# Two more weight tiles between the attention loop and the first gather, issued by GpSimd

## The chip, the cores and the metric

The kernel runs on one core of a Trainium2 chip. The metric is the device time of one execution in microseconds (us). The engines of the core are TensorE (PE; its weight loads are PEld), VectorE (DVE), ScalarE (ACT), GpSimd (POOL) and SyncE (SP); transfers run on 16 DMA engines, fed by a hardware queue (q1, issued by SyncE here) and a software queue (q0, issued by GpSimd).

## The reference

Eight batches of eight heads run an attention with a block-causal mask (576 tokens, head size 64, blocks of 64); the result, 4608 tokens of 512, goes through a mixture of eight experts, of which each token uses one, and each expert keeps at most 80 tokens.

```python
attn = softmax(where(block_i >= block_j, q @ k.T / 8, -1e9)) @ v     # (8, 8, 576, 64)
x = attn.transpose(0, 2, 1, 3).reshape(4608, 512)
logits = x @ w_gate                                                  # 8 experts
expert_idx, gate_w = argmax(logits), softmax(logits) at the argmax
for e in range(8):
    tok_idx = the 80 tokens of expert e with the largest gate_w
    out[tok_idx] = gate_w[tok_idx] * (relu(x[tok_idx] @ w1[e]) @ w2[e])
```

All other rows of the output are zero.

## The kernel before

**The loop.** Two heads make a pair; 32 pairs are taken through the turns of a loop that is written out by hand (lines 40 to 166): loads five turns ahead, transposes, scores, maxima, exponentials (`soft`), transposed probabilities (`back`), values, and the transposition of the result (`flip`). The tables give the order on every engine. The exponentials lie in two sets of tiles, `Pt[0]` and `Pt[1]`, used by even and odd pairs in turn, so the last pair, 31, uses `Pt[1]`. The last turn (table `LAST`) holds only the second half of pair 31's work: its scores and exponentials are made in the turn before. After each batch of four pairs its part of `xs`, the tokens in DRAM, is stored by SyncE (lines 387 to 393), and GpSimd makes a product `sp` (line 463) that TensorE turns (line 472) and VectorE copies to the table `Wt` (line 478), from which the tokens are selected. The product of the last batch but one comes after the loop (`while not turns: t()`, line 770), that of the last batch is made by VectorE.

**The weights.** Each expert has an up tile (`w1`) and a down tile (`w2`) of 2 MB; 16 tiles in the order of `wlist` (line 316): up 0, up 1, down 0, up 2, down 1, up 3, down 2, up 4 and so on. Three buffers (`wp`) are filled during the loop, by GpSimd in DMAs of 512 and 256 KB (line 332). Three more (`fwa`) lie in the memory that the loop's pools of the right side used; they come after `att.close()`. The later ones (`fwc`, `fwb`) come after the selection, and from the tenth tile on buffers are used again. Before the change one tile, up 2, is sent by SyncE (line 337) between the loop and the first gather, behind the stores of the last batch. All further ones wait for the second gather (`fetches[HOLD]`, lines 1019 and 1024).

**The selection and the experts.** VectorE and GpSimd find 80 tokens for each expert; the list is `gi` (line 924). GpSimd issues eight gathers (`xg`, line 934) from `xs`; VectorE divides (`xn`, line 1032), TensorE transposes (line 1052), multiplies with the up tile (line 1043) and the down tile (line 1096), VectorE scales (line 1100) and GpSimd scatters (line 1105). While the selection runs, TensorE is kept busy with filling matmuls on `identr` (line 680). Behind the loop the order on the engines is set by a scheduler, except where `issue_after` ties two instructions.

```python
    for e in range(E):
        fetch = pool.indirect_dma_start(
            out=xg[e], out_offset=None, in_=xs[:, :],
...
    weights(1, fetches[HOLD])
```

Of the kernel before, what the change touches and what calls it, by code (L numbers as in the profile page):

```python
# [7 lines left out]
F32 = mybir.dt.float32  # L8
# [10 lines left out]
P = 128  # L19
BLK = 64  # L20
NT = 5
FW0, FWA, FWC, FWB = 3, 3, 1, 2
WARM = [8, 12, 6, 9, 24]
START_WARM = 6
NCAND = 12
# [7 lines left out]
WIDE = {"78": 512, "56": 512, "34": 320, "12": 256, "08": 3 * BLK}  # L33
# [136 lines left out]
def tile_attn_moe(ctx, tc, q, k, v, w_gate, w1, w2, capacity, out, xs=None, dbg=None):  # L170
    nc = tc.nc
    B, H, S, D = q.shape
    NTOK, DM = out.shape
    E, _, F = w1.shape
# [20 lines left out]
    att = ExitStack()  # L195
    right = dict(side="right")
    pb = att.enter_context(tc.tile_pool(name="pb", bufs=1, **right))
# [38 lines left out]
    def clear(i, eng=nc.gpsimd):  # L236
        if ov is not None:
            if 0 <= i < nz:
                return eng.dma_start(ov[i], zero.rearrange("p (r d) -> p r d", r=2))
        elif i == 0:  # L240
            for j in range(NTOK // BLK):
                nc.sync.dma_start(out[j * BLK:(j + 1) * BLK, :], zero[0:BLK, 0:DM])
# [62 lines left out]
    def constants3():  # L305

        nc.vector.tensor_tensor(iota_c16, sameR, iota_c, op=ALU.mult)
        nc.vector.tensor_reduce(iota_r, iota_c16, axis=AX.X, op=ALU.add)
        nc.gpsimd.tensor_copy(cf, ci)
        nc.vector.scalar_tensor_tensor(cap, cf[:, 1:2], 4294967296.0, cf[:, 0:1], op0=ALU.mult, op1=ALU.add)  # L310
        nc.vector.tensor_tensor(caplt, iota_p, cap, op=ALU.is_lt)

    nw, loaded = 0, None
    wpools = [wp] * FW0
# [4 lines left out]
    def weights(n, after=None):  # L319
        for _ in loads(n, after):  # L320
            pass

    def loads(n, after=None):

        nonlocal nw, loaded
        for _ in range(n):
            src, e = wlist[nw]
            w_ = wpools[nw % len(wpools)].tile([P, KP * F], F32, name="w")
            nw += 1
            wt_[src is w2, e] = w_ = w_.rearrange("p (a f) -> p a f", f=src.shape[2])  # L330
            if nw <= FW0:
                yield from (nc.gpsimd.dma_start(w_[:, a], src[e][a * P:(a + 1) * P]) for a in range(w_.shape[1]))
                continue
            with ExitStack() as order:
                if loaded is not None:
                    order.enter_context(tc.issue_after(loaded.ins))
                load = loaded = nc.sync.dma_start(w_, src[e].rearrange("(a p) f -> p a f", p=P))
            if after is not None:
                tc.add_manual_dep(load.ins, after.name, mybir.DependencyInfo(
                    mybir.DependencyClass.Sync, mybir.DependencyReason.DATA))  # L340

    Pt = [{u: pb.tile([P, 2, w], F32, name=f"P{u}_{i}") for u, w in WIDE.items()} for i in range(2)]

    QT = [pb.tile([P, S], F32, name=f"qt{i}") for i in range(2)]

    VT = [pb.tile([P, 2, D], F32, name=f"vt{i}") for i in range(4)]

    ld = att.enter_context(tc.tile_pool(name="ld", bufs=4, **right))  # L350
    qk = att.enter_context(tc.tile_pool(name="qk", bufs=2, **right))
    attp = ExitStack()
    psp = [attp.enter_context(tc.tile_pool(name=f"psp{i}", bufs=1, space=PSUM)) for i in range(8)]

    def banks(use, where=BANKS):
        return [psp[i].tile([P, 512], F32, name=f"bank{i}") for i in where[use]]
# [134 lines left out]
    class Pair:  # L491
# [11 lines left out]
        def load(self):  # L503

            b, h0 = self.b, self.h0
            self.nat = [ld.tile([P, S // 32, 32], F32, name=f"ld{x}") for x in range(2)]
            for x in (0, 1) if self.i < 2 else (1, 0):
                for h in range(2):
                    for i in range(2):
                        r = slice(h * D + 32 * i, h * D + 32 * i + 32)  # L510
                        eng = nc.sync
                        if h == 1 and (self.i == 0 or x == 1 and self.i > 4):
                            eng = nc.gpsimd if self.i else nc.scalar
                        eng.dma_start(self.nat[x][r], (q, k)[x][b, h0 + h, :, 32 * i:32 * i + 32]  # L514
                                                      .rearrange("(g r) d -> r g d", r=32))

        def load_v(self):
# [3 lines left out]
            for h in range(2):  # L521
                eng.dma_start(self.vn[:, h], v[b, h0 + h, 0:512].rearrange("(j p) d -> p j d", p=P))  # L522
            self.vt = VT[self.i % 4]
            eng.dma_start(self.vt[BLK:P], v[b, h0:h0 + 2, 512:576].rearrange("h p d -> p h d"))

        def prep(self, x):
# [3 lines left out]
            if x == 1:  # L530
                self.T[1] = t
                return
            self.T[0] = q_ = QT[self.i % 2]
            tb, qb = (y.rearrange("p (b r) -> p b r", r=BLK) for y in (t, q_))
# [137 lines left out]
    def warm(n, wt, after=None):  # L672

        if not n:
            return
        with ExitStack() as order:
            if after is not None:
                order.enter_context(tc.issue_after(after.ins))
            for i in range(n):
                nc.tensor.matmul(wt.rearrange("p (a c) -> p a c", c=P), lhsT=identr,  # L680
                                 rhs=identr.unsqueeze(1).broadcast_to([P, 4, P]), start=(i == 0), stop=(i == n - 1))
# [50 lines left out]
    late = ExitStack()  # L732
    tw = dict(reuse_waits="tile")
# [4 lines left out]
    with tc.manual_schedule():  # L738
        warm(WARM[0], banks("g")[0])
        early = loads(FW0)  # L740
        for i in range(-LEAD, n):
            if i == -1:
                nc.sync.dma_start(ci, capacity.bitcast(U32).partition_broadcast(P))
                for h in range(2):
                    nc.sync.dma_start(wgd[h * D:(h + 1) * D, :, h * E:(h + 1) * E], wg_v[h])

            for _ in range(min(4, nz - kept - cleared) if i >= n - 5 else 0):
                clear(cleared, nc.sync)
                cleared += 1
            if i == 1 - LEAD:  # L750
                nc.scalar.activation(early_exp, ramp[:, 2, 0:1], AF.Exp)
                constants()
            if i == -1:
                constants2()
            if i == 1:
                constants3()
            if i >= 2 and i % 3:
                next(early, None)
            for d, what, *args in FIRST if i == -1 else AHEAD if i == -2 else TURN if i < n - 1 else LAST:
                if what in slots_:  # L760
                    slots_[what]()
                elif 0 <= i + d < n and not (what == "flip" and n - NP <= i + d < n - 2):
                    getattr(pairs[i + d], what)(*args)
            if n - NP <= i + valued < n - 2:
                pairs[i + valued].flip()
            if i >= flipped and (i - flipped) % NP == NP - 1 and i - flipped < n - 1:
                enqueue(batches[(i - flipped) // NP])
        for _ in early:
            pass
        while not turns:  # L770
            t()
        bt = batches[B - 1]
        pairs[n - 2].flip()
        for _ in bt.recip():
            pass
        bt.store_sums()
        to, from_ = pairs[n - 1].out.pop("V0")
        pairs[n - 1].take("V1", "v")
        nc.scalar.copy(to[:, 0], from_[:, 0])
        nc.vector.tensor_copy(to[:, 1], from_[:, 1])  # L780
        att.close()
        fwa = late.enter_context(tc.tile_pool(name="fwa", bufs=FWA, **right, **tw))
        wpools += [fwa] * FWA
        lt = bt.logits_of()
        pairs[n - 1].flip()
        bt.store_x()
        weights(1)
        bt.logits_out(lt)
        bt.logits2()
        bt_, mark = turns.pop(0)  # L790
        bt_.turn2(banks("av")[0])
        mark()
        for _ in (*bt.products(), *bt.shift()):
            pass
        bt.expo()
        while small:
            t()
        found, weighed = bt.first_of(), bt.weight()
        for g_ in (found, found, found, weighed, found, weighed, weighed):
            next(g_)  # L800
        bt.turn(nc.vector, 2)
        bt.turn2(banks("L")[0])
        for _ in bt.placed():
            pass
# [8 lines left out]
    pool = nc.gpsimd  # L813
# [50 lines left out]
    HOLD = 1  # L864
# [64 lines left out]
    xg, fetches = [], []  # L929
# [10 lines left out]
    for k, ins in enumerate((bt_.last, bt.last, ranked, picked)):  # L940
        warm(WARM[1 + k], wt[:, k % 2], ins)

# [77 lines left out]
    with tc.issue_after(loaded.ins):  # L1020
        while cleared < nz:
            loaded = clear(cleared, nc.sync)
            cleared += 1
    weights(FWA - 2 + FWC + FWB, fetches[HOLD])

    def divide(dst, src):

# [296 lines left out]
```

## Time and profile before

| what | us |
|---|---|
| median of 3 runs | 396.84 (396.63 to 399.62) |
| the profiled execution | 397.45, of it the span of the trace 395.7 |
| busy: TensorE, VectorE, ScalarE, GpSimd | 374.4, 285.3, 290.7, 171.9 |
| moved by DMA | 84.40 MB, 213 GB/s on the mean |

The span goes from the first to the last instruction. Busy times are sums over the span; a busy TensorE need not be at its peak. A "share" of DMA is the mean busy share of the 16 engines; in loaded stretches it reaches a little over 1. Where a share is multiplied by the length of its stretch, the unit is called share-us. Rows of stretches give the stretch, its length, the busy us (and instructions) of PE, PEld, DVE, ACT and POOL, the granted clock of TensorE (1.00 is 2.4 GHz), the DMA share and GB/s. In rows of a timeline the first number is the start from the span's start, the second the length; in brackets stands the idle time of the engine ahead of it and what ended it.

### The profile page before, as it was taken

The page shows a single profiled execution, that of the slowest core. Times are in us where ns is not written, and L with a number is a line of the kernel's source. Part 1 is how long each engine was busy: PE and PEld are TensorE (multiplying, and loading weights), DVE is VectorE, ACT ScalarE, POOL GpSimd, SP SyncE. Part 2 cuts the span into 40 slices and gives each one's busy share as a digit, 9 for nine tenths or more (in the row PEclk, how much of TensorE's full clock was granted, in tenths as well). Part 3 has the DMA queues.
Part 4 walks back from the last instruction along what each step waited for, and adds up shares of the span by engine and source line. Part 5 has one row for each costly group of instructions (what it writes and reads, how often), then busy time and mean ns, then how long its engine had stood idle before and what let it go on. Part 6 is the DMA issues. An engine that isn't in the chain of part 4 may idle for free. (4 is left out here: it accounts for less than half of the span.)

```text
span 395.7 us, 15123 instructions
## 1 busy us (share of the span) xinstructions
PE 374.4 (95%) x5963; PEld 254.8 (64%) x5963; DVE 285.3 (72%) x812; ACT 290.7 (73%) x886; POOL 171.9 (43%) x333
## 2 busy tenths in 40 slices
PE   5899999999999999999999999998899899999991
PEld 3566766766766766766667667666578745666551
DVE  5879899999999998999999999999764220100000
ACT  1799999999999999999999999999122122333231
POOL 6246664575665567556467544510147010000010
PEclk9999999999999999999999999999999999999997
DMA  9979999899999999999999998999477999999801
GB/s 125 151 125 189 137 183 180 167 214 111 186 170 241 161 136 235 156 156 214 129 153 213 176 151 170 374 383 272 104 244 226 355 398 397 393 398 395 306 22 36
DMA packets 169917, 84.40 MB, mean 213 GB/s; under 512 B 132573, under 2 KB 151869, under 8 KB 169840
## 3 DMA queue, kind: packets, MB, share of 16 engines
q1 hardware_dynamic: 158352, 61.80, 72.5%
q0 software_dynamic: 9120, 21.27, 23.4%
q8 instruction: 49, 0.80, 1.0%
q10 hardware_dynamic: 2368, 0.30, 0.6%
q14 instruction: 28, 0.23, 0.3%
HBM read 63.21 MB, written 20.33 MB: 211 GB/s over the span
## 5 line engine op out<-in xcount | busy, mean ns | idle before, releaser
L600 ACT ACTIVATE P<-bank,negm 128x512 f32<-128x512 f32 (+3 forms) x320 | 158.7, 583 | 11.1 <-DVE negm L589 6.2
L553 PE MATMUL bank<-T,qt 64*128 64x320 f32 (+3 forms) x512 | 98.7, 495 | 1.0 <-DVE PT L670 0.8
L589 DVE TENSOR_REDUCE negm<-bank 128x1 f32<-128x320 f32 (+2 forms) x192 | 83.7, 475 | 8.5 <-PE bank L579 8.4
L652 PE MATMUL bank<-PT,vn 128*64 128x64 f32 (+3 forms) x1280 | 88.1, 293 | 0.6 <-ACT PT L670 0.6
L670 ACT COPY PT<-bank 128x512 f32<-128x512 f32 x158 | 82.6, 669 | 3.6 <-PE bank L634 3.2
L536 POOL TENSOR_SCALAR qt<-T 128x128 f32<-128x128 f32 (+2 forms) x96 | 31.1, 341 | 106.6 <-DVE T L529 106.6
L652 PEld LDWEIGHTS bank<-PT,vn 128*64 128x64 f32 x1280 | 56.3, 137 | 27.1 <-ACT PT L670 4.1
L600 ACT ACTIVATION_READ_ACCUMULATOR P<-bank,negm 128x1 f32 x256 | 70.8, 276 | 0.0
L634 PEld LDWEIGHTS bank<-ident,P 64*128 64x128 f32 (+1 forms) x1600 | 58.9, 137 | 11.9 <-issue 6.3
L634 PE MATMUL bank<-ident,P 64*128 64x64 f32 (+1 forms) x1600 | 64.7, 226 | 1.1 <-ACT P L600 0.6
L553 PEld LDWEIGHTS bank<-T,qt 64*128 64x128 f32 x512 | 46.8, 187 | 27.8 <-ACT PT L670 14.5
L589 DVE TENSOR_REDUCE raw<-bank 128x1 f32<-128x64 f32 (+1 forms) x128 | 52.5, 445 | 2.4 <-PE bank L553 1.6
L529 DVE STREAM_TRANSPOSE T<-ld 128x576 f32<-128x576 f32 x64 | 49.6, 774 | 3.0 <-DMA ld<-in_q_dram 1.7
L522 POOL DMA_DIRECT2D vn<-in_v_dram x58 | 46.0, 799 | 1.6 <-PE bank L658 1.1
L1100 DVE SCALAR_TENSOR_TENSOR y<-av,comb,yt 80x512 f32<-80x512 f32 (+1 forms) x8 | 5.6, 696 | 51.5 <-ACT yt L1099 50.7
L1043 PE MATMUL ps<-xsT,w 128*64 128x80 f32 x1024 | 38.7, 234 | 2.4 <-issue 1.8
L1043 PEld LDWEIGHTS ps<-xsT,w 128*64 128x64 f32 x1024 | 36.6, 137 | 6.0 <-issue 4.7
L1105 POOL DMA_INDIRECT out_dram<-y,si x8 | 7.4, 926 | 74.2 <-DVE y L1100 74.2
L1096 PE MATMUL av<-w,hT 128*32 128x512 f32 (+3 forms) x320 | 39.1, 553 | 0.0
L514 POOL DMA_DIRECT2D ld<-in_k_dram x54 | 37.5, 704 | 3.5 <-DMA ld<-in_q_dram 2.9
L1099 ACT ACTIVATE yt<-ps,gfar 32x512 f32<-32x512 f32 (+2 forms) x18 | 11.4, 635 | 26.0 <-PE ps L1096 25.8
L1066 ACT ACTIVATE hT<-ps 128x320 f32<-128x320 f32 x16 | 7.0, 437 | 30.6 <-PE ps L1043 30.6
(177 smaller groups left out, 435.3 us busy)
## 6 DMA issues: line engine op xcount, KB each, us to landing
w<-in_moe_w_dram SPq DMA_DIRECT2D x13, 2048.0 KB, 21.6
xs<-Y SPq DMA_DIRECT2D x32, 288.0 KB, 5.8
out_dram<-zero SPq DMA_DIRECT2D x18, 512.0 KB, 7.6
ld<-in_q_dram SPq DMA_DIRECT2D x126, 72.0 KB, 5.5
vn<-in_v_dram POOLq DMA_DIRECT2D x58, 128.0 KB, 5.4
ld<-in_k_dram SPq DMA_DIRECT2D x72, 72.0 KB, 5.2
w<-in_moe_w_dram POOLq DMA_DIRECT2D x8, 512.0 KB, 7.2
ld<-in_k_dram POOLq DMA_DIRECT2D x54, 72.0 KB, 6.1
```

What stands on the lines that cost most here:

```text
L514: eng.dma_start(self.nat[x][r], (q, k)[x][b, h0 + h, :, 32 * i:32 * i + 32] .rearrange("(g r) d -> r g d", r=32))
L522: eng.dma_start(self.vn[:, h], v[b, h0 + h, 0:512].rearrange("(j p) d -> p j d", p=P))
L529: nc.vector.transpose(t, self.nat[x].rearrange("p g d -> p (g d)"))
L536: nc.gpsimd.tensor_scalar(qb[:, to], tb[:, of], scalar1=SCALE, scalar2=1.0, op0=ALU.mult, op1=ALU.mult)
L553: nc.tensor.matmul(s[h][:, c:c + n], lhsT=q_[:, P * t - BLK:P * t + BLK], rhs=k_[:, 0:n], start=(c == 0 and g != "2"), stop=(g == "1"))
L589: nc.vector.tensor_reduce(to[:, b, h:h + 1], self.s[g][h][:, c:c + n], axis=AX.X, op=ALU.max, negate=True)
L600: nc.scalar.activation(Pt[self.i % 2][u][:, h, c1:c1 + n], self.s[g][h][:, c:c + n], AF.Exp, bias=self.negm[:, t, h:h + 1], scale=1.0, acc ...
L634: nc.tensor.transpose(pt[c][0:cols.stop - cols.start, n_ * BLK:(n_ + 1) * BLK], row[u][r, h, cols], ident[r, r])
L652: nc.tensor.matmul(a4[r] if c0 is None else av[r, BLK * c0:BLK * (c0 + b1 - b0)], lhsT=self.vn[:, h, j, :], rhs=self.PT[:, h, row, b0:b1]. ...
L670: (nc.scalar.copy if (eng or TAKE[x]) == "a" else nc.vector.tensor_copy)(*self.out.pop(x))
L1043: yield nc.tensor.matmul(dst(b)[64 * c:64 * (c + 1)], lhsT=w_[:, a, col:col + 64], rhs=x_[:, a], start=(a == 0), stop=(a == n - 1))
L1096: last = nc.tensor.matmul(to[col:col + s1 - s0, c0:c1], lhsT=hT[:, a, s0:s1], rhs=w_[:, a, c0:c1], start=(a == ends[0]), stop=(a == ends[1 ...
```

## The change

The weights function lets GpSimd issue the first five tiles instead of the first three (`FW0 + SOON`, with `SOON = 2`). The two more, up 2 and down 1, are issued right behind the loop, ahead of `while not turns: t()`. For this the loop's right-side pools are closed there, and laid out in another order: first the tiles that are read for the last time in the last turn but one (`Pt[0]`, `QT`, the loaded q and k, their transposes `T`), then, in the pools `ld` and `pb1`, the values and `Pt[1]`, which the last turn still reads. SyncE's single tile behind the last batch's stores is now up 3. Behind the gathers two tiles fewer are sent.

```diff
+SOON = 2
...
-            if nw <= FW0:
+            if nw <= FW0 + SOON:
                 yield from (nc.gpsimd.dma_start(w_[:, a], src[e][a * P:(a + 1) * P]) for a in range(w_.shape[1]))
                 continue
...
-    Pt = [{u: pb.tile([P, 2, w], F32, name=f"P{u}_{i}") for u, w in WIDE.items()} for i in range(2)]
-
+    def turned(i, pool):
+        return {u: pool.tile([P, 2, w], F32, name=f"P{u}_{i}") for u, w in WIDE.items()}
+
+    Pt = [turned(0, pb)]
     QT = [pb.tile([P, S], F32, name=f"qt{i}") for i in range(2)]
 
-    VT = [pb.tile([P, 2, D], F32, name=f"vt{i}") for i in range(4)]
-
+    nats = att.enter_context(tc.tile_pool(name="nats", bufs=4, **right))
+    qk = att.enter_context(tc.tile_pool(name="qk", bufs=2, **right))
     ld = att.enter_context(tc.tile_pool(name="ld", bufs=4, **right))
-    qk = att.enter_context(tc.tile_pool(name="qk", bufs=2, **right))
+    pb1 = att.enter_context(tc.tile_pool(name="pb1", bufs=1, **right))
+    Pt.append(turned(1, pb1))
+    VT = [pb1.tile([P, 2, D], F32, name=f"vt{i}") for i in range(4)]
...
-            self.nat = [ld.tile([P, S // 32, 32], F32, name=f"ld{x}") for x in range(2)]
+            self.nat = [nats.tile([P, S // 32, 32], F32, name=f"ld{x}") for x in range(2)]
...
         for _ in early:
             pass
+        att.close()
+        fwa = late.enter_context(tc.tile_pool(name="fwa", bufs=FWA, **right, **tw))
+        wpools += [fwa] * FWA
+        weights(SOON)
         while not turns:
             t()
...
         nc.vector.tensor_copy(to[:, 1], from_[:, 1])
-        att.close()
-        fwa = late.enter_context(tc.tile_pool(name="fwa", bufs=FWA, **right, **tw))
-        wpools += [fwa] * FWA
         lt = bt.logits_of()
...
-    weights(FWA - 2 + FWC + FWB, fetches[HOLD])
+    weights(FWA - SOON - 2 + FWC + FWB, fetches[HOLD])
```

GpSimd's instructions at the end of the loop, before the change (`qt` is the scaled q of the last pair, `sp` the product of the last batch but one):

```order
L536 TENSOR_SCALAR qt_143<-T_5571 128x128
L536 TENSOR_SCALAR qt_143<-T_5571 128x64
L536 TENSOR_SCALAR qt_143<-T_5571 128x384
L463 TENSOR_TENSOR sp<-Gm,sameE 128x320
L892 CAST RI<-sameE 128x12x8
```

The same place after the change, from the second of the new DMAs on, with the counters that each waits for (DMASW are those of the software queue):

```order
L333 DMA w<-in_moe_w_dram 128x1024 [waits DMASW6_49]
L333 DMA w<-in_moe_w_dram 128x1024 [waits DMASW7_49]
L333 DMA w<-in_moe_w_dram 128x1024 [waits DMASW0_49]
L333 DMA w<-in_moe_w_dram 128x512 [waits DMASW1_49,DVE_49,Activation_49]
L333 DMA w<-in_moe_w_dram 128x512 [waits DMASW2_49]
L333 DMA w<-in_moe_w_dram 128x512 [waits DMASW3_49]
L333 DMA w<-in_moe_w_dram 128x512 [waits DMASW4_49]
L333 DMA w<-in_moe_w_dram 128x512 [waits DMASW5_49]
L333 DMA w<-in_moe_w_dram 128x512 [waits DMASW6_49]
L333 DMA w<-in_moe_w_dram 128x512 [waits DMASW7_49]
L333 DMA w<-in_moe_w_dram 128x512 [waits DMASW0_49]
L469 TENSOR_TENSOR sp<-Gm,sameE 128x320 [waits DVE_49]
```

Twelve DMAs, four of the up tile and eight of the down tile, now stand between the last `qt` and `sp`.

SyncE's instructions from the last batch's stores on, before:

```order
L393 DMA xs<-Y 32x18x128 x4
L337 DMA w<-in_moe_w_dram 128x4x1024
L337 DMA w<-in_moe_w_dram 128x8x512
L239 DMA out_dram<-zero 128x1024 x2
L337 DMA w<-in_moe_w_dram 128x4x1024
L337 DMA w<-in_moe_w_dram 128x8x512
L337 DMA w<-in_moe_w_dram 128x4x1024
L337 DMA w<-in_moe_w_dram 128x8x512
L337 DMA w<-in_moe_w_dram 128x4x1024
L337 DMA w<-in_moe_w_dram 128x8x512
L1130 TENSOR_LOAD bad_i
```

And after:

```order
L399 DMA xs<-Y 32x18x128 x4
L338 DMA w<-in_moe_w_dram 128x4x1024
L338 DMA w<-in_moe_w_dram 128x8x512
L240 DMA out_dram<-zero 128x1024 x2
L338 DMA w<-in_moe_w_dram 128x4x1024
L338 DMA w<-in_moe_w_dram 128x8x512
L338 DMA w<-in_moe_w_dram 128x4x1024
L338 DMA w<-in_moe_w_dram 128x8x512
L1137 TENSOR_LOAD bad_i
```

Two weight tiles are gone from this queue; the rows that remain read alike but are two tiles further in `wlist`.

TensorE at the end of the expert stage, before (`ps` and `xsT` are the up layer, `pm`, `av` and `hT` the down layer; `pm` belongs to the last expert):

```order
L1096 MATMUL av<-w,hT 16x512 x2
L1043 MATMUL ps<-xsT,w 64x80 x21
L1096 MATMUL pm<-w,hT 32x384 x2
L1096 MATMUL pm<-w,hT 16x384
L1096 MATMUL av<-w,hT 32x512 x2
```

And after:

```order
L1103 MATMUL av<-w,hT 16x512 x2
L1050 MATMUL ps<-xsT,w 64x80 x64
L1103 MATMUL av<-w,hT 32x512 x2
L1103 MATMUL av<-w,hT 16x512
L1103 MATMUL ps_7138<-w,hT 32x512
```

The last expert's up layer is no longer split, and the first three matmuls of its down layer have gone behind those of the expert before it.

## Rows read from the trace of the kernel before

**Rows 1.** The page: the span in 40 equal slices, busy tenths and GB/s.
```profile
span 395.7 us, 15123 instructions
...
ACT  1799999999999999999999999999122122333231
...
GB/s 125 151 125 189 137 183 180 167 214 111 186 170 241 161 136 235 156 156 214 129 153 213 176 151 170 374 383 272 104 244 226 355 398 397 393 398 395 306 22 36
```
**Rows 2.** Timeline of TensorE: its three waits from 299 us on.
```profile
300.58 0.64 PE L1043 MATMUL ps<-xsT,w 128*64 128x80 f32 x12 [0.51 <-ACT xsT L1053]
...
314.54 1.47 PE L1043 MATMUL ps<-xsT,w 128*64 128x80 f32 x36 [1.77 <-issue]
...
376.45 0.52 PE L1096 MATMUL pm<-w,hT 128*32 128x384 f32 x3 [0.85 <-SPq L1137]
```
**Rows 3.** Line 337: the last weight DMA, issue in ns, landing in us.
```profile
L337 SPq DMA_DIRECT2D w<-in_moe_w_dram x1: 3740/3740/3740, 352.1 to 352.1; - x1
DMA to landing us min/median/max: 24.2/24.2/24.2
```
**Rows 4.** Busy us and instructions, granted clock, DMA share, GB/s, 340 to 370 us.
```profile
340.00:370.00 30.00, 30.00 (x594) 20.74 (x597) 3.05 (x7) 9.08 (x17) 2.74 (x3) 1.00 1.04 394
```
**Rows 5.** Line 934: first and last gathers, landing; the stretch of its first bytes.
```profile
L934 POOL DMA_INDIRECT xg<-xs,gi x1: 1132/1132/1132, 295.3 to 295.3; - x1
...
DMA to landing us min/median/max: 3.2/3.2/3.2
...
L934 POOL DMA_INDIRECT xg<-xs,gi x4: 957/958/1042, 300.6 to 304.5; - x4
...
DMA to landing us min/median/max: 7.5/7.7/7.8
...
297.00:298.00 1.00, 1.00 (x6) 0.84 (x5) 0.00 (x0) 0.00 (x0) 0.75 (x1) 1.00 0.61 175
```
**Rows 6.** Timeline: the first gather's use on VectorE, SyncE's last stores.
```profile
298.57 0.89 DVE L1032 TENSOR_TENSOR xn<-xg 80x128 f32<-80x128 f32 x4 [4.14 <-DMA xg<-xs,gi]
...
281.45 3.80 SPq L393 DMA_DIRECT2D xs<-Y  x4
```
**Rows 7.** Stretches as in rows 4, around the end of the loop.
```profile
258.00:270.00 12.00, 12.00 (x202) 8.70 (x198) 10.82 (x27) 11.25 (x34) 1.07 (x4) 1.00 1.03 389
270.00:278.00 8.00, 6.99 (x130) 5.00 (x128) 7.86 (x26) 6.54 (x23) 0.29 (x1) 1.00 0.81 202
278.00:282.00 4.00, 3.43 (x49) 1.71 (x47) 3.02 (x10) 1.17 (x3) 0.71 (x2) 1.00 0.08 6
282.00:295.00 13.00, 11.72 (x100) 8.92 (x101) 9.91 (x51) 2.92 (x14) 2.82 (x12) 1.00 0.85 251
```
**Rows 8.** Timeline: GpSimd before and at `sp`, TensorE's scores, VectorE's sums.
```profile
277.71 0.80 POOL L463 TENSOR_TENSOR sp<-Gm,sameE 128x320 f32<-128x320 f32 x1 [12.97 <-DVE Gm L455]
...
268.38 1.99 PE L553 MATMUL bank<-T,qt 64*128 64x512 f32 x12
282.32 0.35 PE L472 MATMUL bank<-sp,sameR 128*32 128x40 f32 x16
...
270.97 0.28 DVE L606 TENSOR_REDUCE sums<-P 128x2 f32<-128x128 f32 x1
```
**Rows 9.** Line 332: GpSimd's weight DMAs in the loop, issue in ns, landing in us.
```profile
L332 POOL DMA_DIRECT2D w<-in_moe_w_dram x16: 568/590/606, 33.4 to 224.2; - x16
...
DMA to landing us min/median/max: 4.6/6.5/8.8
```
**Rows 10.** Timeline of VectorE: the copy to `Wt`, the list of the gathers.
```profile
284.27 0.22 DVE L478 COPY Wt<-bank 128x40 f32<-128x40 f32 x1
294.25 0.17 DVE L924 TENSOR_REDUCE gi<-ps 80x8 int32<-80x16 f32 x1 [0.38 <-PE ps L920]
```
**Rows 11.** DMA queues from 306 to 312 us: packets, MB, share.
```profile
q1 hardware_dynamic: 531, 1.27, 70.6%
q0 software_dynamic: 234, 0.58, 34.0%
```

## The prediction

> **What bounds the kernel now.** I read the busy shares by slice first [rows 1]: after the loop (from about 280 us) ScalarE falls to a fifth or so, and in slices 33 to 37 the DMA engines move 393 to 398 GB/s, which looks like a limit by weights. Whether it is one, waits tell, so I read TensorE's from 299 us on [rows 2]: it waits three times, 3.1 us in all. One of 0.51 us is the hand-over of the first expert's transposed tokens. One of 1.77 us at 312.8 us waits for nothing that the trace names ("issue"). One of 0.85 us at 375.6 us is the last weight tile: issued at 352.1 us, landed 24.2 us later, at 376.3, and the matmul starts at 376.45 [rows 2, 3]. From 340 to 370 us TensorE is busy 30.00 of 30 us at full clock while the DMA share is 1.04 [rows 4]. So weights arrive only just in time, but matmuls set the end. A third place matters: the first gather is issued at 295.31 us, lands 3.2 us later, and VectorE starts the first expert at 298.57, after 4.14 us of waiting for it [rows 5, 6]. Everything in the expert stage hangs behind this landing. The filling matmuls of line 680 cover TensorE meanwhile.
>
> **What is free.** The stretches show an almost empty DMA from 278 to 282 us (share 0.08) and part use around it [rows 7]. That is the room for the two tiles. GpSimd does nothing in the 12.97 us ahead of 277.71 [rows 8].
>
> **The change, part by part.**
>
> *Twelve DMAs on GpSimd.* The order shows four for up 2 and eight for down 1, ahead of GpSimd's last `sp` product. The same kind of DMA took 568 to 606 ns to issue and 4.6 to 8.8 us to land [rows 9]: 12 x 0.59 = 7.1 us of GpSimd. They can start when pair 31's score matmuls are done, since the first buffer lies over q and k tiles (`T`) that these read: 270.37 us (268.38 + 1.99); the second lies over probability set 0, which VectorE reads last at line 606, until 271.25 [rows 8]. The built program has eight completion counters for this queue (DMASW0 to 7), so the ninth to twelfth DMA each wait for the first to fourth to land. The fourth is issued by 272.8 and lands by 281.6 at 8.8 us; the twelfth is then issued by 282.2. Behind it waits `sp` (0.80 us), and behind `sp` TensorE's line 472 at 282.32, whose result VectorE copies at 284.27 [rows 8, 10]. 282.2 + 0.80 + 0.35 = 283.4: covered, with 0.9 us over. Price 0; upper bound 1 us if the landing takes 10.7 us instead of 8.8.
>
> *SyncE.* It loses two weight issues and sends up 3 where it sent up 2, behind the last batch's stores (281.45 + 3.80 = 285.25) [rows 6]. SyncE is on no path here: 0.
>
> *The DMA engines from 270 to 300 us.* This is the term that decides. A tile is 2.097 MB; at 394 GB/s it takes 5.32 us at a share of 1.04, so 5.5 share-us, two tiles 11.1. Share times length over the stretches from 270 to 295 gives 0.81 x 8 + 0.08 x 4 + 0.85 x 13 = 6.5 + 0.3 + 11.05 = 17.85 share-us before [rows 4, 7]. With the two tiles it is 28.9, and at the largest share a loaded stretch shows, 1.03 (258 to 270) [rows 7], that lasts 28.1 us from 270, so up 3 moves until about 298. Before, the gather had the DMA to itself: the whole of its landing took 3.2 us. The first gather's bytes move in the microsecond from 297, 1.7 us after its issue [rows 5]; it will meet the end of that tile. Bounds: 0 if the bytes slip through; and the gathers that met a full weight stream, which landed after 7.5 to 7.8 us instead of 3.2, 4.5 us more [rows 5]. Between them I go by what is still ahead of it: from 297 to 298 by the sum above, to 299.2 if the hardware queue keeps two thirds of a shared stretch, as from 306 to 312 us (70.6% against 34.0%) [rows 11]: 1 to 2.2 us. I take +1.5.
>
> *The stores.* The gathers may start when the last batch's stores are in. With two thirds of the time they take: batch 6, 6.5 share-us from 270, until about 279; batch 7, as much again from 282.3, at 0.7 until 291.6: ahead of the gather's 295.3 [rows 5, 7, 11]. Price 0.
>
> *After the first gathers.* Ten weight tiles remain instead of twelve: the stream is 2 x 5.32 = 10.6 us ahead. The last wait of 0.85 us has no cause left. The reordered rows on TensorE (the last expert's up layer together, none of it split off before the end) would take away a wait on ScalarE at the same place, but that is the same 0.85. Price -0.85. The order of VectorE moves eight divisions (0.89 us a group of four [rows 6], so 1.8 us) ahead of `dsb`; the matmul that needs it stands 16 rows, 32 matmuls of the trace, later: the 36 there take 1.47 us, so 1.3 us [rows 2], and the stall of 1.77 us at that place covers the rest. Price 0; 0.5 if the stall goes.
>
> *The loop.* The pools are put in another order, but with the same counts of buffers; no engine's order changes there. 0.
>
> Sum: +1.5 - 0.85 = +0.65 us on a span of 395.7. The profiled execution took 397.45 us, the runs' median is 396.84; I add the sum to the median: **397.5 us**. A measurement of this kernel can tell about 1%, 4 us, from no change.
>
> **Rivals.**
>
> *A. Stores last (slower).* If each DMA engine takes turns, one piece of a store against one piece of a weight, the small pieces lose. A batch's store (line 393) has 2304 pieces of 512 B, 144 on each of 16 engines; the two tiles have 32 pieces of 4 KB and 64 of 2 KB per engine. A store piece costs 6.5 share-us / 144 = 45 ns. 96 rounds take 11.1 + 4.3 = 15.4 share-us, 15 us at 1.03 from 272.1, where the first bytes follow the first issue by the 1.7 us of rows 5: the tiles are done at 287, with 96 store pieces and the 37 of before 272.1 (0.81 x 2.1 = 1.7 share-us) out of 288. The other 155 take 155 x 45 ns / 0.81 = 8.6 us: stores end at 295.6. The first gather goes out about 0.6 us late and meets the whole of up 3: 4.5 + 0.6 - 0.85 = +4.2, **401.1 us**. It decides from the point where stores end after 294.4 us, when the gather's list is ready [rows 10]. For it: the gathers of small pieces did suffer 4.5 us [rows 5]. Against it: from 306 to 312 us, 531 hardware-queue packets went against 234 of the software queue, not one to one [rows 11]. The Trainium skill, "DMA: Bandwidth & Descriptors", section on queues, rings and completion order, says that each engine goes round the queues packet by packet; taken as one piece against one piece that is this rival and 401.1 us, while rows 11 give 397.5. The filling matmuls would then end some 4 us ahead of the first expert, and a lower clock at its start, which no row prices, could come on top.
>
> *B. The weight stream is the real limit (faster).* If busy matmuls hide a pace set by DMA, 10.6 us come back, less 1.5: about **387.7 us**. For it: share 1.04 and a landing at 376.3 with the use at 376.45. Against it: no wait on weights in between, and 30.00 of 30 us busy [rows 2, 4].
>
> *C. No meeting, and the 1.77 us go too.* The stall at 312.8 us falls in a saturated stretch; if it comes from DMA and the changed order moves it away, and the gather meets nothing: -0.85 - 1.77 = -2.6, **394.2 us**. For it: it is no wait for data, and in the same stretch gathers land late [rows 5]. Against it: the DMA is as full at that time afterwards.
>
> *D. GpSimd late.* The upper bound above: +1 us on the selection, but a later gather also meets less of the tile, so at most 398.5.
>
> **Numbers.** Forecast with its own spread (396 to 399): 0.50. C 0.20, D 0.06, A 0.19, B 0.05. Only B is faster by over 1% (0.05), A slower (0.19), the rest, 0.76, within. The range reaches from C to A with the bounds rounded out: 394.0 to 401.2; it leaves out B and about half of A.
>
> **What would show it.** Right: GpSimd's weight DMAs issue from 270.4 to about 282 and `sp` still ends before TensorE's line 472 hurts; the share from 278 to 282 goes from 0.08 to about 1; the first gather lands after 4 to 5.5 us; the wait before the last second-layer matmuls is gone; full DMA ends about 10 us earlier while TensorE's busy stretch keeps its length. A shows in the first gather's issue after 296 and a landing above 7 us, B in an expert stage (first up layer at 300.58 to the end) shorter by more than the waits of rows 2. Wrong would be: the twelve DMAs waiting long past 282, which moves the whole selection, or a stall of TensorE that follows the full DMA elsewhere.

## The result and the profile after

The changed kernel runs in 399.99 us (median of 5, 399.19 to 400.98), the kernel before beside it in 398.09 us (5 runs): ratio 1.0055, 95% interval 1.0032 to 1.0078. A second comparison on another chip (a2_after_again, below) gives 1.0059 (1.0034 to 1.0084). So the change costs 0.6%, some 2.3 us: within 1%, as forecast. The time is 2.5 us above the predicted 397.5; half of that lies in the kernel before, whose median was 396.84 in the three runs that the forecast started from and is 398.09 here.

The profiled execution took 399.99 us, of it a span of 398.2 (before 395.7, [rows 1]). The page of the kernel after, first line and the slices:

```profile
span 398.2 us, 15146 instructions
...
GB/s 126 149 134 184 149 184 170 194 195 137 180 190 211 149 140 226 152 159 222 127 171 224 151 147 276 378 386 265 366 251 211 352 393 399 393 399 278 20 18 22
```

The weight stream now ends in the 37th slice (about 366 us), one slice earlier than in [rows 1], where the 38th still moved 306 GB/s. The hole after the loop is filled, but time was not gained. The timeline of the kernel after shows why; GpSimd first:

```profile
270.73 4.34 POOL L333 DMA_DIRECT2D w<-in_moe_w_dram  x8 [6.22 <-issue]
277.43 0.54 POOL L333 DMA_DIRECT2D w<-in_moe_w_dram  x1 [2.36 <-DMA w<-in_moe_w_dram]
280.28 0.54 POOL L333 DMA_DIRECT2D w<-in_moe_w_dram  x1 [2.31 <-DMA w<-in_moe_w_dram]
281.73 0.54 POOL L333 DMA_DIRECT2D w<-in_moe_w_dram  x1 [0.91 <-DMA w<-in_moe_w_dram]
283.18 0.54 POOL L333 DMA_DIRECT2D w<-in_moe_w_dram  x1 [0.91 <-DMA w<-in_moe_w_dram]
283.73 0.80 POOL L469 TENSOR_TENSOR sp<-Gm,sameE 128x320 f32<-128x320 f32 x1
```

Eight DMAs go out at once; each of the last four waits for an earlier one to land, and `sp` behind them starts at 283.73 instead of 277.71 [rows 8]. TensorE's product with `sp`, its filling matmuls and the copies to `Wt`, after:

```profile
284.58 0.49 PE L478 MATMUL bank<-sp,sameR 128*32 128x40 f32 x16 [2.41 <-POOL sp L469]
285.01 4.20 PE L686 MATMUL ps<-identr 128*128 128x512 f32 x12
289.14 0.35 PE L478 MATMUL bank<-sp,sameR 128*32 128x40 f32 x16
...
285.15 0.23 DVE L484 COPY Wt<-bank 128x40 f32<-128x40 f32 x1 [0.55 <-PE bank L478]
289.56 0.23 DVE L484 COPY Wt<-bank 128x40 f32<-128x40 f32 x1 [2.41 <-PE bank L478]
```

The first copy is only 0.88 us later than before (284.27, [rows 10]). But twelve filling matmuls stand behind the first product, and they now start at 285.01 and take 4.20 us; before they started at 282.60 and took 3.01 (timeline of before, the same places):

```profile
282.60 3.01 PE L680 MATMUL ps<-identr 128*128 128x512 f32 x12
286.08 0.52 PE L472 MATMUL bank<-sp,sameR 128*32 128x40 f32 x16 [0.47 <-DVE sp L463]
```

So the second product comes at 289.14 instead of 286.08. The fills are slower since the granted clock fell to half (1.2 GHz) after TensorE had stood nearly still. Stretches of after, columns as in [rows 4]: TensorE is busy 0.18 of the 2.5 us ahead, and has clock 0.50 behind them; before it was 1.00 throughout [rows 7].

```profile
282.00:284.50 2.50, 0.18 (x5) 0.04 (x1) 2.24 (x7) 0.00 (x0) 1.57 (x4) 0.94 1.06 375
284.50:287.50 3.00, 2.92 (x22) 2.35 (x23) 1.89 (x11) 0.24 (x1) 0.23 (x2) 0.50 1.12 332
```

The list `gi` is ready at 297.18 instead of 294.25 (+2.93), the first gather goes out at 297.64 instead of 295.31 (+2.33), and VectorE starts on its tokens at 300.82 instead of 298.57 (+2.25). Yet TensorE's first matmul for expert 0 starts at 303.51 instead of 300.58, the full 2.93 us later. Between the list and that matmul stand 24 filling matmuls, with the transposes of the first tokens right behind them. Timeline of before, then of after:

```profile
294.07 5.71 PE L680 MATMUL ps<-identr 128*128 128x512 f32 x24
299.62 0.44 PE L1052 MATMUL pm<-ident,xn 80*128 80x80 f32 x4
```

```profile
297.00 5.71 PE L686 MATMUL ps<-identr 128*128 128x512 f32 x24
297.18 0.17 DVE L931 TENSOR_REDUCE gi<-ps 80x8 int32<-80x16 f32 x1 [0.38 <-PE ps L927]
297.64 1.12 POOL L941 DMA_INDIRECT xg<-xs,gi  x1 [3.67 <-DVE gi L931]
300.82 0.89 DVE L1039 TENSOR_TENSOR xn<-xg 80x128 f32<-80x128 f32 x4 [3.46 <-DMA xg<-xs,gi]
302.55 0.44 PE L1059 MATMUL pm<-ident,xn 80*128 80x80 f32 x4
```

The transposes come when the fills end, after the four divisions of the first expert are done (at 299.46 before and 301.71 after). So expert 0's start hangs on the list by way of these fills, and the landing of the gather had time to spare in both kernels. No run changed the number of these 24.

TensorE's waits from 299 us on in the kernel after, against [rows 2]:

```profile
303.51 2.44 PE L1050 MATMUL ps<-xsT,w 128*64 128x80 f32 x64 [0.52 <-ACT xsT L1060]
310.63 3.81 PE L1050 MATMUL ps<-xsT,w 128*64 128x80 f32 x102 [0.36 <-issue]
317.42 2.57 PE L1050 MATMUL ps<-xsT,w 128*64 128x80 f32 x68 [1.50 <-issue]
```

The wait of 0.85 us for the last weight tile is gone; the pause of 1.77 us is now 1.50. Sum: 2.93 - 0.85 - 0.27 = +1.8; the small pause of 0.36 us has a counterpart before, inside a group of rows. The last scatter is issued 1.62 us later (390.11 against 388.49), and the span ends 2.5 us later: another 0.9 us lies behind the last scatter (see the end).

### The profile page after: what moved, and what is told of

Its sections match the earlier page's. It is cut to its first block, busy times and chain, and to the rows that moved or that the text cites. A ratio compares the mean times of both kernels' runs of the same rounds, so it can differ in the third digit from the quotient of the medians.

```text
span 398.2 us, 15146 instructions
## 1 busy us (share of the span) xinstructions
PE 374.5 (94%) x5963; PEld 253.0 (64%) x5963; DVE 285.5 (72%) x812; ACT 290.7 (73%) x886; POOL 178.2 (45%) x345
## 5 line engine op out<-in xcount | busy, mean ns | idle before, releaser
L1103 PE MATMUL av<-w,hT 128*32 128x512 f32 (+2 forms) x320 | 39.0, 554 | 0.0
L1103 PE MATMUL ps<-w,hT 128*32 128x512 f32 (+2 forms) x72 | 29.1, 547 | 0.0
```

What stands on the lines that cost most here:

```text
L1103: last = nc.tensor.matmul(to[col:col + s1 - s0, c0:c1], lhsT=hT[:, a, s0:s1], rhs=w_[:, a, c0:c1], start=(a == ends[0]), stop=(a == ends[1 ...
```

## The experiments

The measurements ran on several chips, each kernel against the kernel before on the same chip. Two of these chips differ from the others: there the kernel before takes 400.9 and 401.4 us instead of 397.7 to 398.1. So ratios are compared, and traces only within one kind of chip.

**Does the order of the pools cost anything?** Only the pools' order and the place where they are closed changed, all DMAs as before (`SOON = 0`).

> The changed order of the buffer pools alone, with every DMA as before. Theory (the layout costs nothing): ratio 1.000 (0.998 to 1.002), list at 294.3, expert 0's first matmul at 300.6, stalls of 1.77 and 0.85 us as before. Rival (the places in SBUF cost something in the loop): the loop's end, read by the last exponent or the last score matmul at 268.4, moves by over 0.5 us, and the ratio is 1.002 or more.

Measured: 1.0011 (0.9993 to 1.0030). The layout costs nothing that can be told.

**The changed kernel again.**

> The changed kernel once more, unedited, on the same chip as the three kernels beside it. Its two readings: ratio to before 1.003 to 1.008 as in its first measurement. Theory (the list of tokens is 2.9 us late because the twelve DMAs hold GpSimd's sp): the trace has sp at 283.7, the list at 297.2 (before: 294.25), the first gather landing in about 3.1 us, expert 0's first matmul at 303.5. Rival (TensorE's issue stalls are a matter of the single execution, not of the kernel): the stalls without a releaser stand at other places or have other lengths than 0.36 and 1.50 us, by over 1 us in sum; in that case the single traces of the other kernels may not be compared to 1 us in expert 0.

Measured: 1.0059 (1.0034 to 1.0084). `sp` at 283.97, first gather issued at 298.16, expert 0 at 304.00: the late list repeats. The rival was right on the pauses: this chip's trace has a slow stretch in expert 0 that the first trace did not have. It goes with the chip and not with the change, since e5, with the engine orders of before, has it on the same chip (last section).

**Is it GpSimd's late `sp`?** Three ways to take `sp` out from behind the four waiting DMAs. Down 1 in four DMAs of 512 KB, so that there are eight in all:

```diff
-    yield from (nc.gpsimd.dma_start(w_[:, a], src[e][a * P:(a + 1) * P]) for a in range(w_.shape[1]))
+    k = 2 if nw > FW0 and src is w2 else 1
+    yield from (nc.gpsimd.dma_start(w_[:, a:a + k], ...) for a in range(0, w_.shape[1], k))
```

> The same two tiles at the same place, but down 1 goes out in four DMAs of 512 KB instead of eight of 256 KB, so that GpSimd's twelve issues are eight and none of them meets a completion counter that is still in use. Theory (GpSimd's product sp stands behind the ninth to twelfth issue, which wait for the first to fourth to land; TensorE waits 2.41 us for sp, its clock falls, and twelve filling matmuls behind it hold the second turn): sp starts at about 277.5 us instead of 283.7, TensorE does not wait for it, the gathers' list is ready at about 294.1 instead of 297.2 and the time falls by about 3 us, to 1 us below the kernel before (its last wait of 0.85 us stays away). Rival (the DMA traffic itself slows the selection or the gathers, whatever GpSimd's order): the list and the time stay within 0.5 us of the changed kernel.

`sp` behind the eighth DMA, the last four behind it:

```diff
-        weights(SOON)
+        soon = loads(SOON)
+        for _ in range(8):
+            next(soon)
         while not turns:
             t()
+        for _ in soon:
+            pass
```

> The changed kernel with GpSimd's product sp behind the eighth of the twelve weight DMAs instead of behind the twelfth; the last four are issued after it. Theory (counters): sp at about 277.5 us, list at 294.1, time about 3 us below the changed kernel, as with eight DMAs; the last four DMAs go out from 278 to 284 as before, so the DMA traffic is unchanged. Rival (traffic): no change from the changed kernel.

`sp` of the last two batches on VectorE (`bt.turn(nc.gpsimd if bt.b < B - 2 else nc.vector)`):

> The changed kernel, but the product sp of the last batch but one is made by VectorE and not by GpSimd; GpSimd's twelve DMAs are untouched. Theory: TensorE does not wait at its turn; VectorE pays some 0.6 us for the product in the last turn, so the list comes at about 294.1 to 294.9 and the time falls by 2 to 3 us against the changed kernel. Rival (traffic): no change, or 0.6 us slower.

Measured: 1.0012 (0.9995 to 1.0029), 0.9989 (0.9974 to 1.0004) and 1.0014 (0.9979 to 1.0050). In all three the list is in time (294.34, 294.50, 294.85 us), and the loss shrinks from 0.6% to 0.1% or nothing. So the late `sp` is the greater part of the loss, and since e2 has the traffic of the changed kernel, it is not the traffic. The changed kernel itself was not run on this chip; e4 below, with `sp` late, has 1.0057 there. The interval of e3 is wide and reaches that figure's. The 1 us below the kernel before that the theory gave for e1 was not reached. The traces of the three also show the meeting of gather and weight tile that the prediction had put into its sum: in e1 VectorE starts on the first expert's tokens at 300.69, 5.5 us after the gather's issue, instead of 3.3. What this costs can't be read on this chip, because expert 0 starts anywhere from 301.26 (e3) to 303.40 (e2), and the slow stretch ends at 306.5 to 307.2 all the same. (The execution of e2 that was traced, 401.68 us, is one of its slowest; the median is 400.44.)

**Is it the fills behind the waiting product?** The changed kernel with four fills there instead of twelve (`WARM[1] = 4`).

> The changed kernel with four filling matmuls instead of twelve between TensorE's two turns of sp. Theory: the first turn is as late as in the changed kernel (284.6 us), but the four fills (1 to 2 us instead of 4.20 at a clock that fell) no longer hold the second, which then waits for VectorE's own product (ready at about 287.1): second turn at about 287.3 instead of 289.1, list and time about 1.9 us earlier than in the changed kernel, about 1 us behind the kernel with eight DMAs. Rival (only the late sp counts, the fills behind it are hidden): no change from the changed kernel.

Measured: 1.0057 (1.0027 to 1.0087); no gain. Timeline of e4:

```profile
284.72 1.19 PE L686 MATMUL ps<-identr 128*128 128x512 f32 x4
286.69 0.59 PE L478 MATMUL bank<-sp,sameR 128*32 128x40 f32 x16 [0.77 <-DVE sp L469]
287.21 2.93 PE L686 MATMUL ps<-identr 128*128 128x512 f32 x6
...
296.10 0.17 DVE L931 TENSOR_REDUCE gi<-ps 80x8 int32<-80x16 f32 x1 [0.38 <-PE ps L927]
```

The second product comes at 286.69, so the twelve fills did hold it. But the low clock only moves to the next six fills (2.93 us instead of 1.67), and the list comes 1.1 us earlier instead of 2.9: fewer fills do not bring back the time that TensorE stood still. Why 1.1 us on the list gave nothing in the time is not shown.

**What does the meeting cost, and what do the early tiles give?** Two tiles early instead of three: in the one up 2 and down 1 on GpSimd in eight DMAs, up 3 behind the second gather; in the other up 2 on GpSimd (`SOON = 1`), down 1 on SyncE.

> Two tiles instead of three ahead of the first gather: up 2 and down 1 in eight DMAs by GpSimd, up 3 behind the second gather with the other late tiles. Theory (the end follows the list and what the first gather meets): sp at 277.7, list at 294.3, the DMA engines empty from about 292, the first gather lands in 3.2 us as before, xn at 298.6, expert 0's first matmul at 300.6, the last wait of 0.85 us gone: ratio 0.998 (0.996 to 1.000). Rival (what comes early is given back in expert 0's up layer, whatever the gather met, by a slow start of TensorE): 1 to 3 us of waits without a releaser in the first 64 matmuls, ratio 1.000 to 1.004.

> One tile on GpSimd (up 2, four DMAs) and one on SyncE (down 1) ahead of the first gather. Theory: GpSimd's four DMAs are issued by 273.5, sp at 277.7, list at 294.3; the SyncE tile, issued behind the last stores at about 285, is in by 293, as up 2 was before; first gather 3.2 us, expert 0's first matmul at 300.6, last wait gone: ratio 0.998 (0.996 to 1.000). Rival (expert 0 starts slowly whenever the DMA was full from 278 to 285): 1 to 3 us of waits without a releaser in expert 0, ratio 1.000 to 1.004.

Measured, on a chip with the slow stretch: 1.0029 (1.0013 to 1.0046) and 1.0017 (0.9989 to 1.0045). Both have the list and the first gather in time (expert 0 at 300.83 and 301.28), and both miss the theory's gain. The reason is in e5 on the same chip: expert 0 loses so much in the slow stretch that TensorE's list of waits holds no wait for a weight tile any more. Where nothing waits for weights, earlier weights give nothing. That e7 is slower than the kernel before, by 0.3%, is not explained by this.

Then three kernels in which also the last three of the eight gathers wait for the first half of expert 0's up layer:

```diff
-    for e in range(E):
...
+    gathers(0, 5)
...
                 with tc.issue_after(last.ins):
                     then()
+                gathers(5, E, last.ins)
```

> The kernel before, with the last three of the eight gathers made to wait for the first 32 matmuls (64 records) of expert 0's up layer; every engine's order is unchanged. In the eight traces taken on the two chips of the experiments, TensorE issues single matmuls 0.7 us apart from about the 38th record of that half layer on, until 0.9 to 1.4 us after GpSimd has issued the last gather. Theory (GpSimd's gather issue holds up TensorE there): the slow stretch is gone, the half layer takes 2.44 us instead of 6 to 8, the clock stays at 1.00, and the kernel is 3 to 5 us faster, ratio 0.988 to 0.993, on a chip that shows the stretch. Rival (the stretch ends when TensorE's next packet on the instruction queue is in, whatever GpSimd does): the stretch stays, ratio 0.998 to 1.002.

> The changed kernel with down 1 in four DMAs (eight on GpSimd, sp not late) and with the same held gathers. Theory: as in the kernel before with held gathers, the slow stretch is gone; the first gather meets up 3 (landing 5 us, expert 0 later by 1 us and a lower clock at its start, 1 to 2 us in all), but the last weight tiles come 10 us earlier, so that the wait for the last one, which should come back when expert 0 is faster, is not there: 0 to 1 us slower than the kernel before with held gathers, ratio 0.990 to 0.995. Rival (stretch independent of GpSimd): ratio 1.000 to 1.004.

> Two early tiles in eight DMAs on GpSimd, up 3 behind the second gather, and the same held gathers. Theory: first gather 3.2 us, expert 0's first matmul at 300.6, slow stretch gone, last wait gone: faster than the kernel before with held gathers by the last wait, 0.5 to 1.5 us, ratio 0.985 to 0.991: the version that should beat both. Rival (stretch independent of GpSimd): ratio 1.000 to 1.004.

> Two early tiles with held gathers once more, unedited. On a chip where the kernel before runs in 400 to 402 us (the slow stretch of expert 0 was there in all eight traces of two such chips): if GpSimd's gather issue is what holds TensorE up, the stretch is gone and the ratio is 0.985 to 0.991; if it is not, the stretch is there and the ratio is 1.000 to 1.004. On a chip where the kernel before runs in 396 to 398 us: no stretch, last wait gone, ratio 0.995 to 0.998 as in its first measurement.

These ran on chips without the slow stretch (before 397.69 and 397.83 us), so what was to be told apart about that stretch stays open, and the gains of 0.5 to 1.5% that the first three expectations gave for its removal did not come. They settle something else, because here the kernels differ by single steps. h0, the kernel before with held gathers: 0.9993 (0.9980 to 1.0006), no change. h1, with up 2, down 1 and up 3 early and `sp` in time (277.99): 0.9984 (0.9964 to 1.0004), where the changed kernel with its late `sp` had 1.0055 on a chip of this kind. h2, with two tiles early: 0.9967 (0.9956 to 0.9979), and again (h3) 0.9955 (0.9934 to 0.9977). **h2 beats both kernels**, the kernel before on the same chip, the changed one by its ratio.

VectorE's first division in h0 and h1, TensorE's first transposes in h1, and the stretch of h1 in which up 3 ends:

```profile
298.48 0.89 DVE L1040 TENSOR_TENSOR xn<-xg 80x128 f32<-80x128 f32 x4 [4.04 <-DMA xg<-xs,gi]
```

```profile
300.24 2.51 DVE L1049 TENSOR_TENSOR xn<-xg 80x128 f32<-80x128 f32 x12 [5.41 <-DMA xg<-xs,gi]
300.58 0.90 PE L1069 MATMUL pm<-ident,xn 80*128 80x80 f32 x4 [0.42 <-DVE xn L1049]
...
293.00:298.00 5.00, 4.51 (x28) 3.64 (x29) 1.45 (x5) 0.16 (x1) 2.13 (x2) 1.00 1.01 389
298.00:299.00 1.00, 1.00 (x6) 0.84 (x5) 0.00 (x0) 0.00 (x0) 0.95 (x1) 1.00 0.69 187
```

Both gathers are issued at the same time (295.33 and 295.31). In h1 the DMA engines are full until 298, and the tokens come 1.76 us later; expert 0 starts at 302.00 instead of 300.56, +1.44 us. Here the transposes do wait for the tokens. Not all of the 1.44 us is the meeting: the list is 0.39 us later in h1 (294.66 against 294.27), and its 24 fills alone would have moved expert 0 by 0.40 us, so the meeting adds about 1.0. In h2, without up 3, the share from 292 to 297 is at most 0.13, and expert 0 starts at 300.84, 0.28 us later than in h0, with a list that is 0.27 us later.

TensorE's wait for the last weight tile stands in h0 (timeline, 0.84 us) and in neither h1 nor h2; h2's waits in full follow it:

```profile
375.83 0.52 PE L1105 MATMUL pm<-w,hT 128*32 128x384 f32 x3 [0.84 <-SPq L1146]
```

```profile
300.84 2.43 PE L1059 MATMUL ps<-xsT,w 128*64 128x80 f32 x64 [0.52 <-ACT xsT L1069]
313.34 1.47 PE L1059 MATMUL ps<-xsT,w 128*64 128x80 f32 x36 [0.68 <-issue]
```

The last scatter is issued at 387.87 in h0, 388.70 in h1, 386.03 in h2. h0 to h2 is 1.84 us: 0.84 the last wait, 0.77 shorter pauses (0.22 and 1.23 in h0, 0.68 in h2), less 0.28 for the later start; 0.5 is left unassigned. These are single traces: in h3, the same kernel as h2, the pauses sum to 0.92 us instead of 0.68.

## Why the prediction was right, and where it was not

**The time.** The forecast of no measurable change by 1% and the range 394.0 to 401.2 held. The mechanism behind 397.5 did not: of its two terms that were not zero, one was right, one did not take place, and a term priced at zero became the largest. That the time still came out near is in part luck: a delay of 2.93 us that was not foreseen stood in for the 1.5 us that were.

**GpSimd, priced 0, bound 1 us: the step that failed.** Most of its parts were right: the start (270.73 against 270.4), the ninth to twelfth DMA waiting for the first to fourth, and even the excess at the first copy, 0.88 us, inside the bound of 1 us for a late landing. Landing took up to 11.0 us, with eight weight DMAs and batch 6's stores under way, not 8.8 [rows 9], so the twelfth issue came at 283.18 instead of 282.2 (line 333 in the trace after, loop and new DMAs together):

```profile
L333 POOL DMA_DIRECT2D w<-in_moe_w_dram x28: 537/573/607, 33.2 to 283.2; - x28
...
DMA to landing us min/median/max: 5.1/6.7/11.0
```

What failed is the stop at that copy: I compared with the moment VectorE copies and forgot what stands on TensorE behind the delayed product, the twelve fills ahead of the second product and their clock. My own sum had `sp` end at 283.0, 0.7 us after the start of TensorE's product before (282.32), so it already made the fills late. An excess of 0.88 us became 2.93 on the list. Rival D had the right mechanism with the wrong size; its price of 1 us on the selection should have been 3. e1, e2 and e3 show that taking `sp` out of the queue brings the list back; e4 shows that the fills alone are not the cure.

**The gather meets the third tile, +1.5 us.** It did not happen in the changed kernel, for the reason that the list was late: its first gather was issued at 297.64, after up 3 was in, and landed in 3.1 us. Where the list is in time (h1), the DMA engines are full until 298, the time that I had worked out, and the first tokens come 1.76 us later, of which about 1.0 reaches expert 0. So the meeting was right for a kernel with `sp` in time, but not that a late landing is passed on in full: I had everything in the expert stage hang behind the landing, while the 24 fills set expert 0's start. Against h1, where the transposes wait for the tokens and the first matmul follows 1.76 us behind the first division, the landing had some 0.3 us to spare before (2.01) and 0.9 after (2.69).

**The last wait, -0.85.** Right: gone in every kernel with two or three early tiles. In the traces h1 against h0 is close to what the sum forecast for the change as a whole: the last scatter is issued 0.83 us later, the forecast was +0.65. That is in part chance, since the pauses of 0.22 and 1.23 us in h0 are 1.29 and 0.68 in h1. The times can't tell the two apart (0.9984 and 0.9993, with intervals that overlap).

**SyncE, stores, layout, `dsb`, 0 each.** The layout is shown by e5. The stores did not hold the first gather: in e1 and h1, with the list in time, it is issued at 295.22 and 295.31, as before. SyncE and `dsb` were not tried by themselves; no wait of TensorE for them stands in the trace after.

**The rivals.** A (stores last, gather lands after 7 us): no, the landing was 3.1 us; the gather's issue after 296 us waited for the list and not for stores. B (the weight stream is the limit): no, from expert 0's first matmul to the last scatter's issue it is 86.6 us instead of 87.9, shorter by little more than the waits that went (0.85 and 0.27). C: the pause of 1.77 us shrank to 1.50, not to 0. It shrinks further, to 0.68, in h2.

## What to carry to other kernels

When an instruction is late, follow it past its first reader: price what is queued behind the reader on its engine, fillers and their clock included, until the next product that the chain needs. Work put into an idle queue must leave that queue before the next thing on it is due; splitting it into no more pieces than go out without waiting (here eight) brought back most of what the change cost. And filling a hole in the DMA helps only as far as something later waits for the bytes: here 0.85 us, so two tiles are enough; a third one meets the first gather, and in the traces that takes back more than the wait was worth (about 1.0 us). Before a transfer is called critical, look at what its reader's engine is doing when it lands: here 24 fillers ended after the tokens had come.

## What the runs showed of the hardware

**Pauses of TensorE that wait for no data.** Weight loads of TensorE in the trace after, between the two pauses marked "issue":

```profile
310.63 3.65 PEld L1050 LDWEIGHTS ps<-xsT,w 128*64 128x64 f32 x102 [0.52 <-issue]
314.37 0.53 PEld L973 LDWEIGHTS <-OH 128*80 128x80 bf16 x12
314.81 0.11 PEld L996 LDWEIGHTS <-ones 128*128 128x128 bf16 x1
314.85 0.62 PEld L1059 LDWEIGHTS pm<-ident,xn 80*128 80x128 f32 x8
315.56 0.26 PEld L1050 LDWEIGHTS ps<-xsT,w 128*64 128x64 f32 x5
317.42 0.69 PEld L1050 LDWEIGHTS ps<-xsT,w 128*64 128x64 f32 x18 [1.60 <-issue]
```

102 + 12 + 1 + 8 + 5 are 128 loads, with as many matmuls 256 instructions, and the count is the same before the change and in h1. Each of these pauses ends 2.5 to 2.8 us after a packet of the instruction queue starts (read in steps of 0.25 us): packets from 304.75 and 311.75 us before, pauses over at 307.48 and 314.54; after, 308.00 and 314.75, over at 310.63 and 317.42; in h1, 307.50 and 313.50, over at 310.05 and 316.02. The page counts 49 such packets and 0.80 MB, 16 KB each. So these pauses look like waits for instructions that come late through full DMA engines; no run took the packets away, so it is not shown. The Trainium skill, "Runtime: NRT & Kernel Launch", section on instruction fetch mechanics, says that instructions come in blocks of 16 KiB, 256 instructions, over a DMA queue of the engine's own, which agrees with these counts; it calls the cost mostly hidden; if these pauses are that cost, up to 1.77 us of it were not hidden here.

**A slow stretch on some chips.** In all eight traces from the two slower chips TensorE goes through part of expert 0's up layer with single matmuls 0.7 us apart (in e1 and e2 only the last two). Timeline of e5, whose engine orders are those of before:

```profile
300.47 1.53 PE L1050 MATMUL ps<-xsT,w 128*64 128x80 f32 x37 [0.52 <-ACT xsT L1060]
302.39 0.23 PE L1050 MATMUL ps<-xsT,w 128*64 128x80 f32 x1 [0.40 <-issue]
303.80 0.23 PE L1050 MATMUL ps<-xsT,w 128*64 128x80 f32 x1 [1.18 <-issue]
304.52 0.23 PE L1050 MATMUL ps<-xsT,w 128*64 128x80 f32 x1 [0.50 <-issue]
305.24 0.27 PE L1050 MATMUL ps<-xsT,w 128*64 128x80 f32 x1 [0.49 <-issue]
305.95 0.29 PE L1050 MATMUL ps<-xsT,w 128*64 128x80 f32 x1 [0.44 <-issue]
306.67 1.85 PE L1050 MATMUL ps<-xsT,w 128*64 128x80 f32 x22 [0.43 <-issue]
```

It ends 0.9 to 1.4 us after GpSimd has issued the last gather, in each of the eight, and in e5 the granted clock is at 0.50 from 306 to 312 us. Whether the gathers cause it is open: the kernels with held gathers did not run on such a chip.

**0.9 us behind the last scatter.** The span ends 7.1 to 7.2 us after the last scatter's issue in the kernels with no or one tile more on GpSimd (before, e5, e6, h0) and 7.9 to 8.2 us after it in all with two. The cause is open.
